# Linformer attention with a max-out FFN on one core: batch 0's k product in one column tile, its prelude reordered, and four output copies moved from ScalarE to VectorE

## The chip, the cores and the metric

The kernel runs on one core of one Trainium2 chip. The metric is the time of one execution in device microseconds. Each run also comes with its span and its mean granted TensorE clock (1.0 is full speed).

"Half clock" below means a stretch in which TensorE's clock is granted at 0.50. In the runs' clock column one such stretch of 3.4 us in 404 us shows as about 0.996. I call a run with a clock under 0.9975 a run with a dip. The clock column has a blind spot: it reads 1.00 until the first recorded change of the clock, so an array that warms up late doesn't count as a dip.

## The reference, cut to what matters

```python
# q, k, v: (8 batches, 8 heads, 1024, 64) fp32; E, F: (64, 1024)
k_proj = np.einsum('ks,bhsd->bhkd', E, k)             # 1024 keys -> 64
v_proj = np.einsum('ks,bhsd->bhkd', F, v)
scores = scale * np.matmul(q, k_proj.transpose(0, 1, 3, 2))
attn = softmax(scores)                                # over the 64
x = np.matmul(attn, v_proj) -> (8192 tokens, 512)
h = np.maximum(np.maximum(x @ w1, x @ w2), x @ w3)    # 512 -> 768
out = h @ w_out                                       # 768 -> 512, fp32
```

The matmuls run in bf16. The three "up" products and the "down" product of the FFN are most of the work: 1152 and 378 matmuls of 512 columns.

## The kernel before

Each batch of 1024 tokens is worked in two chunks of 512. While TensorE multiplies the FFN of one batch, the attention of the next is slipped in between. Batch 0 has nothing to hide behind, so its attention is a prelude: it runs while the first weights are still arriving. The prelude works two "duos" of four heads each for q and k, and four pairs of heads for the values. `idle(n)` issues n fill matmuls whose results nobody reads; they keep the array active. `at(us)` only tells the program's own model of time, which places instructions; it makes no wait on the chip.

```python
    def proj(b, kv, t, heads, width):                 # two 64-column tiles of the array
        for si in range(SI):                          # SI = 8
            for hh in range(2):
                nc.tensor.matmul(
                    out=t[hh * HALF:(hh + 1) * HALF, 0:width],
                    lhsT=efT[:, si, (kv - 1) * KP:kv * KP],
                    rhs=qkv[b][kv][:, heads[hh], si, :],
                    start=(si == 0), stop=(si == SI - 1),
                )
        ...
    def idle(n):
        t, ns = bank()
        for _ in range(n):
            nc.tensor.matmul(out=t, lhsT=warm[:, 0:P], rhs=warm, start=True, stop=True)
        free[ns[0]] = pe(n * MM)
    ...
    def k_duo(u):
        t, ns = bank()
        proj(0, 1, t, (slice(4 * u, 4 * u + 2), slice(4 * u + 2, 4 * u + 4)), 2 * D)
        kp0[u] = att.tile([P, 2 * D], BF16, name="kp0")
        copy("v", kp0[u], t[:, 0:2 * D], ns, 0.3)

    def kt_duo(u):
        ...
        nc.tensor.transpose(out=t[:, 0:P], in_=kp0[u], identity=ident)
        ...
    # the prelude, from the second k duo on
    k_duo(1)
    idle(2)
    kt_duo(1)
    at(14.1)
    v_pair(0)
    for g in (2, 3):
        exps(0, g, *C0, scores(0, g, *C0))
    x(0)
    at(15.5)
    v_pair(1)
    z(2)        # sums, then ln and exp on ScalarE: the softmax's divisor
    z(3)
    x(1)        # values times weights, then the scaling on VectorE: xT
    idle(1)
    at(17.4)
    ...
    # the first FFN chunk: six products w1, ct by ct, with work slipped in
                up_first({
                    (0, 0, 5): [lambda: v_pair(2)],
                    (0, 1, 2): [lambda: x(2)],
                    (0, 1, 5): [lambda: v_pair(3), ld(1)],   # ld(1): load batch 1
                    ...
            # after each chunk: down products; the copy out of PSUM on VectorE or ScalarE
            for tt in range(SPC):
                down(b, ch, tt, "v" if (b, ch) == (0, 0) else "s")
                behind(ch, NJT + tt)
```

The softmax here doesn't subtract the row's maximum and nothing guards it: scores larger than these inputs give would overflow.

## Time and profile before

| | before |
|---|---|
| time of the three timed runs | 405.33, 405.44, 405.68 us |
| time, span, clock of the execution that was traced | 406.75 us, 405.0 us, 0.996 |
| TensorE busy | 392.0 us, 97% |
| first up matmul | 18.97 us |
| half clock | 19.2 to 22.6 us |
| batch 1's first up products wait for their input | 0.67 us at 78.07 us |

The page's summary of the kernel before: span, busy time by engine, then the granted clock in tenths and the busy share of the DMA engines in 40 slices of 10.1 us.

```profile
span 405.0 us, 5872 instructions
PE 392.0 (97%) x2331; PEld 178.8 (44%) x2374; DVE 200.1 (49%) x309; ACT 191.1 (47%) x278; POOL 31.7 (8%) x44
PEclk9989999999999999999999999999999999999999
DMA  9999999948927994991898119950510202020202
```

TensorE is the limit of the whole. In the first eight slices, though, the DMA engines are over 90% busy as well. The 8 in the clock row is most of the half clock.

The timeline of TensorE around the first weights, in the kernel before (start in us, length in us, engine, line, operation, and in brackets how long the engine sat idle before it and what ended that):

```profile
17.42 0.39 PE L380 MATMUL banks<-warm 128*128 128x512 bf16 x1
18.97 2.54 PE L496 MATMUL banks<-xT,w_sb 128*128 128x512 bf16 x6 [1.16 <-DMA w_sb<-in_moe_w_dram]
21.30 1.06 PE L425 MATMUL banks<-v_t,efT 128*128 128x128 bf16 x8
```

L380 is a fill, L496 the up product, L425 a value pair. Six up matmuls take 2.54 us here.

The windows view of the kernel before, by microsecond (columns: length, busy time and count of PE, PEld, DVE, ACT, POOL, then the granted clock, the DMA share and GB/s):

```profile
18.00:19.00 1.00, 0.03 (x1) 0.03 (x2) 0.30 (x1) 0.97 (x2) 0.00 (x0) 1.00 1.23 202
19.00:20.00 1.00, 1.00 (x3) 0.36 (x4) 0.00 (x0) 0.64 (x2) 0.79 (x1) 0.61 1.24 207
20.00:21.00 1.00, 1.00 (x4) 0.42 (x3) 0.00 (x0) 0.00 (x0) 0.63 (x2) 0.50 1.18 209
21.00:22.00 1.00, 1.00 (x9) 0.72 (x8) 0.00 (x0) 0.00 (x0) 0.35 (x2) 0.50 1.16 206
22.00:23.00 1.00, 0.78 (x6) 0.44 (x4) 0.29 (x1) 0.00 (x0) 0.91 (x2) 0.69 1.17 212
```

The timeline of the end of batch 0, kernel before, ScalarE first and then TensorE. L99 is the copy of an output tile, L233 and L239 are the ln and exp of batch 1's divisor.

```profile
71.67 0.59 ACT L99 COPY o_sb<-banks 128x512 f32<-128x512 f32 x1
74.18 0.57 ACT L99 COPY o_sb<-banks 128x512 f32<-128x512 f32 x1
74.64 1.03 ACT L233 ACTIVATE zl<-banks 128x1024 f32<-128x1024 f32 x1
75.70 1.06 ACT L239 ACTIVATE zi<-zl 128x1024 f32<-128x1024 f32 x1
75.30 2.11 PE L496 MATMUL banks<-xT,w_sb 128*128 128x512 bf16 x9
78.07 1.24 PE L496 MATMUL banks<-xT,w_sb 128*128 128x512 bf16 x4 [0.67 <-DVE xT L250]
```

The copies lie in ScalarE's way to the last exp; the scaling on VectorE (L250) follows that exp, and TensorE waits for it.

### The profile page before, as it was taken

How to read it: one execution, taken by the hardware profiler on the slowest of the kernel's cores; microseconds unless marked ns; L12 is line 12 of the kernel's file. 1: busy time of each engine (PE TensorE's matmuls, PEld its weight loads, DVE VectorE, ACT ScalarE, POOL GpSimd, SP SyncE). 2: the span in 40 equal slices, each digit the busy share in tenths (PEclk: the TensorE clock that was granted, in tenths of full speed). 3: DMA queues.
4: the chain of work that ended last, by engine and by line, in shares of the span. 5: the costliest groups of instructions: out<-in, count | busy, mean ns of one | idle time of the engine just before them, and what ended most of it. 6: DMA issues, size and time to landing. Idle time of an engine off the chain costs nothing.

```text
span 405.0 us, 5872 instructions
## 1 busy us (share of the span) xinstructions
PE 392.0 (97%) x2331; PEld 178.8 (44%) x2374; DVE 200.1 (49%) x309; ACT 191.1 (47%) x278; POOL 31.7 (8%) x44
## 2 busy tenths in 40 slices
PE   7899999999999999999999999999999999999996
PEld 3444444344444535444544445444544444444443
DVE  2337764462655527537353655625464363525251
ACT  2611538724763366555544555437535556432322
POOL 7340010002000100200200002000000000000000
PEclk9989999999999999999999999999999999999999
DMA  9999999948927994991898119950510202020202
GB/s 151 206 206 207 229 198 184 232 106 124 256 36 209 177 238 106 141 247 29 211 188 178 49 29 238 205 154 2 139 71 1 104 2 104 2 104 0 105 0 104
DMA packets 62667, 53.33 MB, mean 132 GB/s; under 512 B 30128, under 2 KB 58288, under 8 KB 62640
## 3 DMA queue, kind: packets, MB, share of 16 engines
q0 software_dynamic: 28512, 28.31, 43.8%
q1 hardware_dynamic: 33984, 24.51, 19.5%
q8 instruction: 18, 0.29, 0.3%
q10 hardware_dynamic: 144, 0.13, 0.1%
q14 instruction: 9, 0.07, 0.1%
HBM read 57.15 MB, written 16.78 MB: 183 GB/s over the span
## 4 chain that ended last, share of the span: by engine, by line
PE 89%; DMA 4%; ACT 2%; issue 2%; POOL 1%; DVE 1%; ACTq 0%; DVEq 0%; POOLq 0%
PE banks L496 61%; PE banks L593 19%; PE banks L220 4%; PE banks L284 3%; DMA w_sb<-in_moe_w_dram 3%; PE banks L200 2%; DVE xT L250 1%; ACT zl L233 1%; ACT zi L239 1%; DMA out_dram<-o_sb 0%; POOL k_t L147 0%; ACT pT L211 0%; PE banks L425 0%; POOL q_t L152 0%; POOL v_t L147 0%
## 5 line engine op out<-in xcount | busy, mean ns | idle before, releaser
L496 PE MATMUL banks<-xT,w_sb 128*128 128x512 bf16 x1120 | 256.1, 380 | 4.3 <-DMA w_sb<-in_moe_w_dram 1.2
L496 PEld LDWEIGHTS <-w_sb 128*128 128x128 bf16 x1152 | 109.9, 98 | 139.2 <-issue 12.3
L558 DVE TENSOR_TENSOR m<-banks,h1s 128x512 f32<-128x512 f32 x90 | 62.1, 689 | 85.1 <-ACT h1s L554 52.7
L554 ACT COPY h1s<-banks 128x512 f32<-128x512 f32 x90 | 52.5, 583 | 89.8 <-PE banks L496 87.7
L593 PE MATMUL banks<-wout_sb,hT 128*128 128x512 bf16 x369 | 84.6, 379 | 1.0 <-issue 0.6
L250 DVE TENSOR_TENSOR xT<-banks,zi 128x1024 bf16<-128x1024 f32 (+1 forms) x36 | 39.8, 1106 | 76.1 <-ACT zi L239 54.6
L506 DVE TENSOR_TENSOR hT<-banks,m 128x512 bf16<-128x512 f32 x90 | 62.3, 692 | 10.7 <-PE banks L496 1.2
L99 ACT COPY o_sb<-banks 128x512 f32<-128x512 f32 (+1 forms) x60 | 34.8, 581 | 52.4 <-PE banks L593 52.4
L593 PEld LDWEIGHTS <-hT 128*128 128x128 bf16 x378 | 36.0, 98 | 45.3 <-issue 2.9
L233 ACT ACTIVATE zl<-banks 128x1024 f32<-128x1024 f32 (+1 forms) x36 | 33.5, 931 | 30.6 <-PE banks L220 29.7
L211 ACT ACTIVATE pT<-banks 128x1024 bf16<-128x1024 f32 (+1 forms) x36 | 33.2, 931 | 14.3 <-PE banks L200 14.3
L239 ACT ACTIVATE zi<-zl 128x1024 f32<-128x1024 f32 (+1 forms) x36 | 34.6, 962 | 1.1
L189 POOL DMA_DIRECT2D q_t<-in_q_dram x7 | 6.2, 880 | 204.3 <-DMA qT<-q_p 142.0
L284 PEld LDWEIGHTS <-efT 128*64 128x64 bf16 x256 | 12.8, 110 | 4.5 <-issue 4.0
L220 PE MATMUL banks<-pT,ones 64*64 64x512 bf16 (+1 forms) x144 | 13.9, 376 | 0.7 <-DVE xT L250 0.3
L200 PE MATMUL banks<-qT,kpT 64*64 64x512 bf16 (+1 forms) x144 | 13.3, 358 | 0.4 <-DVE m L558 0.3
L220 PE MATMUL banks<-pT,vp 64*64 64x512 bf16 (+1 forms) x144 | 13.3, 356 | 0.1
L99 DVE CAST vp<-banks 64x256 bf16<-64x256 f32 (+1 forms) x18 | 7.1, 396 | 9.0 <-PE banks L425 5.2
L220 PEld LDWEIGHTS <-ones 64*64 64x64 bf16 x144 | 4.4, 103 | 14.6 <-issue 14.2
L99 DVE COPY q_p<-q_t 128x1024 bf16<-128x1024 bf16 x28 | 10.0, 420 | 0.0
L380 PE MATMUL banks<-warm 128*128 128x512 bf16 x22 | 8.2, 499 | 1.5 <-DVE warm L170 1.2
L284 PE MATMUL banks<-k_t,efT 128*64 128x256 bf16 (+1 forms) x144 | 8.7, 263 | 0.7 <-DMA k_t<-in_k_dram 0.7
(46 smaller groups left out, 94.6 us busy)
## 6 DMA issues: line engine op xcount, KB each, us to landing
out_dram<-o_sb SPq DMA_DIRECT2D x30, 512.0 KB, 3.0
q_t<-in_q_dram POOLq DMA_DIRECT2D x7, 1024.0 KB, 9.6
k_t<-in_k_dram POOLq DMA_DIRECT2D x7, 1024.0 KB, 13.9
v_t<-in_v_dram POOLq DMA_DIRECT2D x7, 1024.0 KB, 19.8
w_sb<-in_moe_w_dram POOLq DMA_DIRECT2D x5, 384.0 KB, 12.4
k_t<-in_k_dram POOLq DMA_DIRECT2D x2, 512.0 KB, 8.7
v_t<-in_v_dram POOLq DMA_DIRECT2D x4, 256.0 KB, 12.0
wout_sb<-in_moe_w_out_dram POOLq DMA_DIRECT2D x1, 768.0 KB, 15.7
```

What stands on the lines that cost most here:

```text
L99: done = {"v": nc.vector.tensor_copy, "s": nc.scalar.copy, "g": nc.gpsimd.tensor_copy}[eng](out=o, in_=i)
L211: nc.scalar.activation(out=pTs[b, g, lo], in_=t, func=AF.Exp, scale=scale)
L220: nc.tensor.matmul(out=t[hp * HALF:(hp + 1) * HALF, c, 0:nsi * HALF], lhsT=w(rows, hp), rhs=p[rows, hp, :], start=True, stop=True,)
L233: nc.scalar.activation(out=zl, in_=t, func=AF.Ln)
L239: nc.scalar.activation(out=zi, in_=zl, func=AF.Exp, scale=-1.0)
L250: nc.vector.tensor_tensor(out=xTs[b][:, g, lo:lo + nsi, :].rearrange("a (c s) p -> a c (s p)", c=2), in0=t, in1=zi, op=ALU.mult,)
L284: nc.tensor.matmul(out=t[hh * HALF:(hh + 1) * HALF, 0:width], lhsT=efT[:, si, (kv - 1) * KP:kv * KP], rhs=qkv[b][kv][:, heads[hh], si, :], ...
L496: nc.tensor.matmul(out=h, lhsT=w_sb[i][:, ct, jt * P:(jt + 1) * P], rhs=xTs[b][:, ct, ch * SPC:(ch + 1) * SPC, :], start=(ct == first), st ...
L506: nc.vector.tensor_tensor(out=o, in0=h, in1=other, op=ALU.max)
L554: nc.scalar.copy(out=h1s, in_=h[0][0])
L558: nc.vector.tensor_tensor(out=m12, in0=h[1][0], in1=h1s, op=ALU.max)
L593: nc.tensor.matmul(out=o_ps, lhsT=hTs[b, ch][:, jt, tt * P:(tt + 1) * P], rhs=wout_sb[:, jt, :], start=(jt == 0), stop=(jt == NJT - 1),)
```

## The change

The intent: the k product of batch 0 issues half the matmuls, value pair 0 covers the wait between the k product and its transpose, fewer fills are needed, and ScalarE is relieved of four output copies at the end of batch 0.

```diff
     def k_duo(u):
         t, ns = bank()
-        proj(0, 1, t, (slice(4 * u, 4 * u + 2), slice(4 * u + 2, 4 * u + 4)), 2 * D)
-        kp0[u] = att.tile([P, 2 * D], BF16, name="kp0")
-        copy("v", kp0[u], t[:, 0:2 * D], ns, 0.3)
+        for si in range(SI):
+            nc.tensor.matmul(
+                out=t[0:KP, 0:4 * D], lhsT=efT[:, si, 0:KP],
+                rhs=k_t[:, 4 * u:4 * u + 4, si, :],
+                start=(si == 0), stop=(si == SI - 1),
+            )
+        pe(0.9)
+        kp0[u] = att.tile([KP, 4 * D], BF16, name="kp0")
+        copy("v", kp0[u], t[0:KP, 0:4 * D], ns, 0.45)
     def kt_duo(u):
...
-        nc.tensor.transpose(out=t[:, 0:P], in_=kp0[u], identity=ident)
+        for gg in range(2):
+            nc.tensor.transpose(
+                out=t[:, gg * KP:(gg + 1) * KP],
+                in_=kp0[u][:, gg * P:(gg + 1) * P], identity=ident[0:KP, 0:KP],
+            )
...
-    idle(11)
+    idle(10)
...
-    idle(5)
+    idle(4)
...
     k_duo(1)
-    idle(2)
+    idle(1)
+    at(14.8)
+    v_pair(0)
     kt_duo(1)
-    at(14.1)
-    v_pair(0)
+    x(0)
     for g in (2, 3):
         exps(0, g, *C0, scores(0, g, *C0))
-    x(0)
-    at(15.5)
+    at(16.1)
     v_pair(1)
+    idle(1)
+    x(1)
     z(2)
     z(3)
-    x(1)
-    idle(1)
-    at(17.4)
+    at(18.2)
...
-                down(b, ch, tt, "v" if (b, ch) == (0, 0) else "s")
+                down(b, ch, tt, "v" if b == 0 else "s")
```

## The prediction

> **What bounds it.** The page gives TensorE 97% of a 405.0 us span, and its granted clock is full (the windows view: 1.00 over 79 to 400 us, TensorE busy 318.0 of 321 us). The change removes no work there, so only the first 80 us can give anything. Three losses there:
>
> 1. Waiting for weights. The timeline has the last fill matmul end at 17.81 us; the first up matmul starts at 18.97 us, after 1.16 us of waiting for the DMA of the first half of w1. The chain of waits gets there through that DMA, not the k products.
> 2. A half clock. The windows view grants 0.61, 0.50, 0.50, 0.69 in the four microseconds from 19 to 23 us: half speed from about 19.22 to 22.62 us, 3.40 us long. The Trainium skill, "TensorE: Matmul & The Clock Gate", section "Part 1: The HAM clock gate", has an activity window of 3413 ns and a halved clock after an idle one; the trace agrees on length and factor. So the window 15.81 to 19.22 us was too idle. Cost: 1.7 us.
> 3. The end of batch 0. At 78.07 us TensorE has waited 0.67 us for xT of batch 1 (VectorE), itself behind a full ScalarE: from 70 to 77 us ScalarE carries four output copies (0.57 us each) between exp and ln.
>
> **What the change does.**
> - k product: twice 16 matmuls of 128 columns in two column tiles (0.64 us a set) become twice 8 of 256 in one tile. From the value products (8 of 128 columns, 0.61 us) I estimate 1.05 us a set. The copy grows from 0.29 to about 0.41 us, the transpose becomes two. Each k chain is some 0.5 us longer.
> - Value pair 0 covers the wait for the second copy; fewer fills. TensorE should finish the prelude near 18.4 us instead of 17.8, still before the weights at 18.95. Loss 1 becomes a wait of 0.4 to 0.6 us, and the up matmuls start when they did.
> - Window 15.81 to 19.22 gets more array time: I count columns streamed for 39% of it before and about 50% after; an earlier window with 48% (8.98 to 12.40) kept the full clock. So probably (0.6) the half clock vanishes. Then up to 1.7 us is gained, less about 0.3 because value pair 2 and the next weights land only just in time: about 1.4 us.
> - Output copies: ScalarE reaches the last ln and exp about 0.5 us earlier; VectorE takes four copies of about 0.68 us in its gaps. xT is ready near 77.5 instead of 78.0: the 0.67 us wait falls to about 0.15. Gain 0.5 us.
>
> **Sum.** With the full clock 405.4 - 1.4 - 0.5 = 403.5 us; without it 404.9. Prediction 403.8 us, range 402.9 to 405.4. Faster by over 2%: 0.01; within 2%: 0.98; slower: 0.01.
>
> **Right or wrong in the profile.** First up matmul at 18.9 to 19.0 us; k product sets near 1.05 us; granted clock 1.00 from 19 to 23 us; the wait for batch 1's xT (near 76 us) under 0.3 us; the same durations from 80 us on.
>
> **What would make it wrong.** The half clock stays (then about 404.9), or moves earlier, since two fills less leave the window 5.6 to 9.0 us emptier (then the prelude is late and the time over 405.5). The k chain passes 18.95 us. The last xT waits behind an output copy on VectorE. Weights or batch 1's values land too late for the gained time.

## More of the kernel before

All runs come from six sittings, five of them on chips whose number is on record (14, 15, 9, 12 and 3). The kernel before was run again in each, and only run times of one sitting are compared; traces are read across sittings.

## The result, and the profile after

The kernel after ran four times: 405.02, 405.19, 405.51 and 406.20 us, median 405.35 us. The kernel before beside it has a median of 405.56 us over four (405.33 to 405.76). The ratio is 0.9998, with a 95% interval of 0.9981 to 1.0016: the same time.

The forecast was 1.6 us less; 0.2 us less was measured. Yet the trace after looks like the forecast come true. The page's summary of the kernel after:

```profile
span 403.2 us, 5841 instructions
PEclk9999999999999999999999999999999999999999
DMA  9999999959907994991799029950510202020202
```

The span fell from 405.0 to 403.2 us and the half clock is gone. The timeline of TensorE around the first weights, kernel after (L506 is now the up product, L435 the value pair):

```profile
18.06 0.39 PE L220 MATMUL banks<-pT,ones 64*64 64x256 bf16 x8
19.54 1.47 PE L506 MATMUL banks<-xT,w_sb 128*128 128x512 bf16 x6 [1.08 <-DMA w_sb<-in_moe_w_dram]
20.84 0.61 PE L435 MATMUL banks<-v_t,efT 128*128 128x128 bf16 x8
```

The up products start 0.57 us later than in the trace before, still waiting for the weights, and six of them take 1.47 us instead of 2.54. The windows view of the kernel after has the clock at 1.00 there:

```profile
19.00:20.00 1.00, 0.47 (x3) 0.23 (x4) 0.05 (x1) 0.94 (x3) 0.22 (x1) 1.00 1.25 209
20.00:21.00 1.00, 1.00 (x8) 0.53 (x7) 0.00 (x0) 0.96 (x2) 1.00 (x2) 1.00 1.17 206
```

The end of batch 0, kernel after: VectorE, then TensorE.

```profile
74.28 0.68 DVE L99 COPY o_sb<-banks 128x512 f32<-128x512 f32 x1
75.28 1.23 DVE L250 TENSOR_TENSOR xT<-banks,zi 128x1024 bf16<-128x1024 f32 x1 [0.32 <-ACT zi L239]
76.42 0.68 DVE L99 COPY o_sb<-banks 128x512 f32<-128x512 f32 x1
74.29 2.10 PE L506 MATMUL banks<-xT,w_sb 128*128 128x512 bf16 x9
76.56 2.75 PE L506 MATMUL banks<-xT,w_sb 128*128 128x512 bf16 x11 [0.17 <-DVE xT L250]
```

The wait for batch 1's xT fell from 0.67 to 0.17 us, and no output copy delays the scaling. So between these two traces 1.8 us were gained, by the mechanisms forecast (though not in the sizes: by the second reading below, 0.97 us before batch 1's value product, where 1.4 was forecast, and 0.8 us after it, where 0.5 was). Between the timed runs 0.2 us were gained. The two can only agree if the traced execution before was not one like its timed runs. The runs' own figures say so: the traced one took 406.75 us with a clock of 0.996, the timed ones 405.33 to 405.68 us. (The clocks of these three timed runs are not on record; later sittings record them.)

A second reading of all traces helps with what follows. From the value product of batch 1 (near 56 us) to its first up product 18.3 us pass in every trace quoted here. From there to the end 329.7 us pass with batch 0's copies on ScalarE and 328.9 us with them on VectorE (329.2 in one of these, h1). So a trace's span is: the start of that value product, plus 18.3 us, plus one of the two numbers. Before: 56.98 + 18.3 + 329.7 = 405.0. After: 56.01 + 18.3 + 328.9 = 403.2.

### The profile page after: what moved, and what is told of

Its sections match the earlier page's. It is cut to its first block, busy times and chain, and to the rows that moved or that the text cites. A ratio compares the mean times of both kernels' runs of the same rounds, so it can differ in the third digit from the quotient of the medians.

```text
span 403.2 us, 5841 instructions
## 1 busy us (share of the span) xinstructions
PE 389.6 (97%) x2314; PEld 178.0 (44%) x2357; DVE 203.1 (50%) x313; ACT 189.4 (47%) x274; POOL 31.6 (8%) x44
## 4 chain that ended last, share of the span: by engine, by line
PE 82%; DMA 11%; ACT 2%; POOL 1%; DVE 1%; issue 1%; DVEq 0%; ACTq 0%; POOLq 0%
PE banks L506 56%; PE banks L603 18%; DMA v_t<-in_v_dram 7%; PE banks L220 4%; DMA w_sb<-in_moe_w_dram 3%; PE banks L284 3%; PE banks L200 2%; DVE xT L250 1%; ACT zi L239 1%; ACT zl L233 1%; DMA out_dram<-o_sb 0%; POOL k_t L147 0%; POOL q_t L152 0%; POOL v_t L147 0%; PE banks L435 0%
## 5 line engine op out<-in xcount | busy, mean ns | idle before, releaser
L506 PE MATMUL banks<-xT,w_sb 128*128 128x512 bf16 x1119 | 254.9, 379 | 3.7 <-DMA w_sb<-in_moe_w_dram 1.1
L506 PEld LDWEIGHTS <-w_sb 128*128 128x128 bf16 x1152 | 109.4, 98 | 138.1 <-issue 10.7
L99 ACT COPY o_sb<-banks 128x512 f32<-128x512 f32 (+1 forms) x56 | 32.6, 581 | 52.2 <-PE banks L603 52.1
L284 PEld LDWEIGHTS <-efT 128*64 128x64 bf16 x224 | 11.6, 110 | 3.3 <-issue 2.7
L99 ACT CAST vp<-banks 64x256 bf16<-64x256 f32 x14 | 5.1, 365 | 8.8 <-PE banks L284 8.6
L380 PE MATMUL banks<-warm 128*128 128x512 bf16 x19 | 7.0, 498 | 1.2 <-DVE warm L170 1.2
## 6 DMA issues: line engine op xcount, KB each, us to landing
v_t<-in_v_dram POOLq DMA_DIRECT2D x7, 1024.0 KB, 18.8
```

The costliest lines, as they stand in the source:

```text
L99: done = {"v": nc.vector.tensor_copy, "s": nc.scalar.copy, "g": nc.gpsimd.tensor_copy}[eng](out=o, in_=i)
L284: nc.tensor.matmul(out=t[hh * HALF:(hh + 1) * HALF, 0:width], lhsT=efT[:, si, (kv - 1) * KP:kv * KP], rhs=qkv[b][kv][:, heads[hh], si, :], ...
L506: nc.tensor.matmul(out=h, lhsT=w_sb[i][:, ct, jt * P:(jt + 1) * P], rhs=xTs[b][:, ct, ch * SPC:(ch + 1) * SPC, :], start=(ct == first), st ...
```

## The experiments

Two theories stand against each other.

- **The base was wrong.** The half clock happened in the execution that was traced but in few of the timed ones, before and after alike. There was little to remove. What is left is the copies' gain and whatever the new prelude costs.
- **The gain was given back.** The half clock was typical before, the change removes it, and the new prelude loses about as much elsewhere, for example by later weights.

All medians and ratios are in one table; the text after it goes run by run. No ratio is beyond 2%; the differences below are finer than that. "Dips" counts runs with a clock under 0.9975. The median of the kernel before in the same sitting stands in the third column.

| run | median us | before us (chip) | ratio [95%] | dips |
|---|---|---|---|---|
| b1_before_again | 405.39 | 405.37 (14) | 0.9992 [0.9975, 1.0008] | 1 of 6 |
| a1_after_again | 405.38 | 405.37 (14) | 0.9989 [0.9972, 1.0006] | 3 of 6 |
| o1_copies_only | 404.80 | 405.37 (14) | 0.9981 [0.9965, 0.9996] | 1 of 6 |
| k1_prelude_only | 405.77 | 405.37 (14) | 1.0005 [0.9989, 1.0021] | 0 of 6 |
| q1_quads_only | 405.98 | 405.21 (15) | 1.0004 [0.9986, 1.0023] | see text |
| r1_order_only | 405.62 | 405.21 (15) | 0.9999 [0.9981, 1.0017] | 0 of 6 |
| f1_copies_and_fills | 404.75 | 405.21 (15) | 0.9979 [0.9960, 0.9998] | 0 of 6 |
| g1_value2_later | 405.09 | 405.21 (15) | 0.9985 [0.9969, 1.0002] | 0 of 6 |
| h1_after_ln_first | 405.84 | 405.38 (9) | 1.0008 [0.9994, 1.0023] | 0 of 6 |
| d1_thin_fills | 404.60 | 405.38 (9) | 0.9985 [0.9968, 1.0002] | 3 of 6 |
| q2_quads_only | 405.55 | 405.38 (9) | 1.0004 [0.9986, 1.0022] | 0 of 6 |
| f2_copies_and_fills | 404.74 | 405.38 (9) | 0.9980 [0.9963, 0.9996] | 0 of 6 |
| p1_after_small_fills | 404.27 | 405.58 (12) | 0.9976 [0.9960, 0.9992] | 1 of 6 |
| p2_after_all_small | 404.90 | 405.58 (12) | 0.9984 [0.9972, 0.9996] | 0 of 5 |
| s2_copies_all_small | 404.54 | 405.58 (12) | 0.9977 [0.9964, 0.9990] | 0 of 5 |
| s3_copies_early_small | 404.69 | 405.58 (12) | 0.9978 [0.9966, 0.9990] | 1 of 5 |
| a2_after_third | 405.24 | 405.98 (3) | 0.9979 [0.9966, 0.9993] | 0 of 5 |
| p3_after_small_fills | 405.49 | 405.98 (3) | 0.9986 [0.9974, 0.9999] | 0 of 5 |

### b1_before_again: the kernel before, unchanged

No edit.

> The kernel before, unedited, run as if it were a new one. Theory A (chance): the half clock near 19 to 23 us falls in some executions of either kernel and misses others, because the window's phase moves against the program; the traced execution of before (406.75 us, mean clock 0.996) was such a one and its timed runs (405.33 to 405.76 us) were not. Then a clock below 1.0 goes with a time near 406.5 us and appears in a minority of these runs, the rest read clock 1.0 and about 405.4 us. Theory B (my prediction): before always has the half clock; then every run of it reads a clock near 0.996 at about 405.4 us.

It is the same program, and its ratio reads 0.9992: differences of 0.1% (0.4 us) are at the edge of what a sitting resolves. Its trace had the full clock and a span of 403.4 us, 1.6 us less than the traced execution that the prediction was built on. In the five sittings the kernel before had a dip in 5 of 53 runs, and b1 in 1 of 6. So the half clock costs the median of the kernel before nothing; at about one run in ten and 1.3 us a dip (406.75 less 405.44) it costs the mean about 0.12 us, by estimate from these numbers. The five dips themselves agree: they took 0.2 to 1.9 us, on average 1.3 us, more than the median of the runs without a dip in their sittings.

### a1_after_again: the kernel after, unchanged

No edit.

> The kernel after, unedited. Theory A: the same minority of runs with clock near 0.996, 1.0 to 1.5 us longer; the other runs 0.3 to 0.5 us shorter than runs of before at clock 1.0, which is the wait for batch 1's xT alone: ratio 0.9988 to 0.9995. Theory B: all runs at clock 1.0 and at least 1.4 us (0.35%) faster than before. Theory C (the prelude costs something): runs at full clock equal to before although the wait for xT is gone, ratio 1.000.

Three of six runs had a dip: 405.51, 405.61 and 405.96 us, against 404.67, 405.00 and 405.25 us without: 0.7 us more on average, and half of the runs where theory A had said a minority and 1.0 to 1.5 us. The traced execution had one too, but at another place. The windows view of this run:

```profile
9.00:10.00 1.00, 1.00 (x7) 0.40 (x4) 0.89 (x2) 0.57 (x1) 0.00 (x0) 0.58 1.38 197
10.00:11.00 1.00, 1.00 (x4) 0.28 (x3) 0.00 (x0) 0.00 (x0) 0.16 (x1) 0.50 1.33 200
11.00:12.00 1.00, 1.00 (x7) 0.82 (x6) 0.00 (x0) 0.00 (x0) 0.41 (x1) 0.50 1.27 207
12.00:13.00 1.00, 1.00 (x5) 0.26 (x3) 0.36 (x1) 0.00 (x0) 0.54 (x1) 0.71 1.27 210
```

Half clock from about 9.2 to 12.6 us: the k product of this execution takes 1.92 us in place of 1.03. The change does not remove the half clock. Over all its runs the kernel after had one in 4 of 15 (1 of 4, 3 of 6, 0 of 5), no rarer than before. This is the first theory's case: there was hardly a half clock in the base to remove, and no sign that the change makes it rarer. Under the second theory most runs of the kernel before would have shown a clock near 0.996.

### o1_copies_only: the copies alone

```diff
-                down(b, ch, tt, "v" if (b, ch) == (0, 0) else "s")
+                down(b, ch, tt, "v" if b == 0 else "s")
```

> Before, with only the output copies of batch 0's second chunk on VectorE. Theory A and C: wait of TensorE for xT before the last slice of batch 1's first matmuls 0.1 to 0.2 us instead of 0.67; time 0.4 to 0.5 us less, ratio 0.9988 to 0.9990; the half clock as often as in before. Theory B: the half clock stays in every run.

404.80 us, ratio 0.9981, an interval that leaves 1 out. From batch 1's first up product to the end 329.70 us (before), 329.68 (b1), 329.63 (k1), 329.68 (r1) and 329.68 (q2) pass with the copies on ScalarE; 328.94 (o1), 328.94 (f1), 328.91 (after), 328.98 (a1), 328.90 (g1) and 328.96 (a2) with them on VectorE. That is 0.74 us, the same each time. The wait for xT accounts for 0.50 of it (0.67 to 0.17 us).

The other 0.24 us lie 230 us later. The chain of waits in b1 has a gap there:

```profile
306.90 1.52 PE banks L496 x7
308.43 0.38 issue
308.80 0.70 DVE hT L506
```

VectorE begins a max 0.38 us after its inputs are ready, for no wait that the profile shows, and a down product waits for it. In o1 the same max follows at once, and its 24 down matmuls take 5.34 us where b1's take 5.58. The timelines of TensorE in b1 and then in o1:

```profile
308.25 5.58 PE L593 MATMUL banks<-wout_sb,hT 128*128 128x512 bf16 x24
307.88 5.34 PE L593 MATMUL banks<-wout_sb,hT 128*128 128x512 bf16 x24
```

It is so in each of the traces compared: k1 and r1 have the gap (5.58 and 5.60 us), f1, d1, after and a1 do not (5.34 us). A hint at the cause: a transfer of 8 KB on an instruction queue (q14, probably that of VectorE, since more instructions on VectorE bring its transfers forward) starts at 309.5 to 310.3 us in the three with copies on ScalarE, right after the gap, and at 305.6 to 307.1 us in the five with copies on VectorE. Four more instructions on VectorE (313 in place of 309) shift where such a transfer falls. This is argued from eight traces, not tested.

### k1_prelude_only: all of the change but the copies

```diff
-                down(b, ch, tt, "v" if b == 0 else "s")     # the kernel after
+                down(b, ch, tt, "v" if (b, ch) == (0, 0) else "s")
```

> After, with the output copies of batch 0's second chunk back on ScalarE, so only the prelude is changed. Theory A: ratio 1.000 within 0.0005. Theory B: 1.4 us faster, 0.9965. Theory C: 0.3 to 0.5 us slower, 1.0008 to 1.0012, with the first up matmul or the weights' landing later than in before.

405.77 us, ratio 1.0005, against 0.9992 for the unchanged program on the same chip. The prelude gains nothing and probably loses a few tenths. Its trace shows one way of losing them. The timeline of TensorE and of ScalarE in k1:

```profile
18.50 0.39 PE L220 MATMUL banks<-pT,ones 64*64 64x256 bf16 x8
18.82 1.74 PE L506 MATMUL banks<-xT,w_sb 128*128 128x512 bf16 x6
20.82 0.61 PE L435 MATMUL banks<-v_t,efT 128*128 128x128 bf16 x8 [0.26 <-ACT zl L233]
20.17 0.60 ACT L233 ACTIVATE zl<-banks 128x512 f32<-128x512 f32 x1
```

The same place in o1, which has the old prelude:

```profile
17.42 0.39 PE L380 MATMUL banks<-warm 128*128 128x512 bf16 x1
18.77 1.47 PE L496 MATMUL banks<-xT,w_sb 128*128 128x512 bf16 x6 [0.95 <-DMA w_sb<-in_moe_w_dram]
20.07 0.61 PE L425 MATMUL banks<-v_t,efT 128*128 128x128 bf16 x8
18.41 0.60 ACT L233 ACTIVATE zl<-banks 128x512 f32<-128x512 f32 x1
```

In k1 the weights were there when the prelude ended; it wins no time by it. Its prelude ends 1.1 us later, so the last ln of pairs 2 and 3 ends at 20.77 us instead of 19.01 and still holds its bank of PSUM (the buffer that matmuls write to) when value pair 2 wants one. The first six up matmuls take 1.74 us instead of 1.47, value pair 2 waits 0.26 us, and the stretch from the first up product to the second q transposes takes 14.50 us instead of 13.80. This costs 0.7 us where the weights come early (k1, a2) and nothing where they come late (after, 13.80 us from a start at 19.54); early and late here mean before and after the end of the prelude. Either way the later of the two, weights or prelude, sets the pace: the loss of the new prelude was hidden in the trace after behind weights that happened to come late. That the bank is the reason is read from the waits; g1 and h1, below, tried to remove this wait and gained nothing that can be told apart from noise.

Not all of the 1.1 us is the new order, though. The fills and the first k product, in k1 and then in o1:

```profile
8.51 1.89 PE L380 MATMUL banks<-warm 128*128 128x512 bf16 x4
10.33 1.17 PE L409 MATMUL banks<-k_t,efT 128*64 128x256 bf16 x8
```

```profile
9.74 0.64 PE L284 MATMUL banks<-k_t,efT 128*64 128x128 bf16 x16 [0.51 <-DMA k_t<-in_k_dram]
```

In k1 four fills take 1.89 us, because the array is cold until 10.6 us (fills step at 0.427 us instead of 0.216; in o1 it is cold until 7.2 us), and the k product begins 0.59 us later than in o1. The clock column shows 0.999 for this run. Of the 19 traces with a clock record only k1 and p2 (10.1 us) warm up this late, and both have the new prelude; the count of dips misses them. So the prediction's risk that fewer fills leave the early window emptier is larger than the dips alone say, though two traces give no rate.

### q1_quads_only and q2_quads_only: the k product by quads (four heads in one column tile), the old order

```diff
     def k_duo(u):
         t, ns = bank()
-        proj(0, 1, t, (slice(4 * u, 4 * u + 2), slice(4 * u + 2, 4 * u + 4)), 2 * D)
+        for si in range(SI):
+            nc.tensor.matmul(out=t[0:KP, 0:4 * D], lhsT=efT[:, si, 0:KP], ...)
...                                   # and the two transposes; all else as before
```

> Before with only the k product by quads (one column tile, two transposes per copy); order, fills and output copies as before. Theory C1 (the longer k chain delays exp and ln on ScalarE and so the prelude, which then ends after the weights have landed): each k set 1.05 us instead of 0.64, its copy 0.42 instead of 0.29, first ln of pairs 2 and 3 about 0.8 us later than in the traces of before with full clock, and 0.3 to 0.5 us slower, ratio 1.0007 to 1.0012. Rival C2 (the new order and the fewer fills are what costs): ratio 1.000.

> The same kernel as the quads-only run, whose profiled execution ran at the half clock from end to end and can't be read. C1: the sets at 1.05 us, ln of pairs 2 and 3 some 0.8 us later than before, first up matmul to the second q transposes 14.2 to 14.5 us unless the weights come late; median 0.3 to 0.7 us above before, as the other 5 runs (405.98 against 405.21 us) suggest. C2: no difference from before.

The traced execution of q1 was useless for its purpose: it ran at half clock from end to end. The groups view, up matmuls, q1 and then q2 (the same kernel on another chip); columns as on the page: count, busy us, mean ns, idle before.

```profile
span 819.8 us, 5886 instructions
L506 PE MATMUL banks<-xT,w_sb 128*128 128x512 bf16 x1152 | 544.5, 676 | 0.0
```

```profile
L506 PE MATMUL banks<-xT,w_sb 128*128 128x512 bf16 x1152 | 257.9, 379 | 1.0 <-DVE xT L250 0.7 <-DMA w_sb<-in_moe_w_dram 0.2
```

821.54 us, once; its other five runs took 405.37 to 406.12 us (clocks of 0.998 to 1.0), and these make the ratio of 1.0004. The clock column says 1.0 for the 821.54 us run and its page has no clock row, so only the durations give it away. Run again as q2: 405.55 us, 1.0004, no such execution. Quads alone gain nothing. In its trace the k products of 1.03 to 1.06 us (0.64 before) leave no mark in the stretch: up at 18.81 us, second q transposes at 32.62 us.

### r1_order_only: the new order and fills, the old k product

It is k1 with the k product and transpose of the kernel before put back.

> After's order, fills and start times with before's k product (two column tiles) and before's output copies. C1: ratio 1.000 or a little under, the first up matmul waits for the weights' DMA again. C2: 0.3 to 0.5 us slower, ratio 1.0007 to 1.0012, and the first fills or transposes at the slow step more often.

405.62 us, ratio 0.9999. The trace starts the up products at 19.31 us after a wait of 1.03 us for the weights. So neither half of the prelude gains alone, and there is no hidden winner among them.

### f1_copies_and_fills and f2_copies_and_fills: the copies, the old prelude, three more fills

```diff
     x(1)
-    idle(1)
+    idle(4)                          # o1 with the wait for the weights filled
     at(17.4)
```

> Output copies on VectorE, before's prelude, and three more fill matmuls in the wait for the first weights (four instead of one, 0.65 us more work in about 1.0 us of wait). Theory A says that the half clock is a matter of how busy a 3.4 us window is: no run of this kernel then reads a clock of 0.996 for a dip near 19 to 23 us, and the median is the 404.7 us of the full-clock runs with the copies on VectorE, ratio about 0.998. Rival: fills do not change the dip; then one run in five reads 0.996 as in before. If the fills delay the first up matmul, 0.1 to 0.3 us slower than with the copies alone.

> The same kernel as the run with copies on VectorE and three more fills, again, as the best so far: median 404.6 to 404.9 us, ratio 0.998, no run with clock under 0.998.

404.75 us on chip 15 and 404.74 us on chip 9, ratios 0.9979 and 0.9980, no dip in 12 runs. This is the best version that I can vouch for: 0.2% (0.8 us) under the kernel before, twice, with an interval that leaves 1 out each time. The kernel after was not run in these two sittings; against the kernel before it averages 0.9989, so this version is probably ahead of it too, by about 0.1%, and a variant of each kind in one sitting agrees (o1 404.80 us, a1 405.38 us on chip 14). It is hardly better than o1 without the fills (0.9981), as it must be if dips are rare. That no run of 12 had a dip shows little by itself: at the 5 in 53 of the kernel before, 12 runs show none about three times in ten.

### d1_thin_fills: o1 with thin fills in the second half of the prelude

```diff
     k_duo(0)
-    idle(2)
+    idle(2, 64)                      # 64 columns in place of 512; so with all eight fills from here on
```

> Output copies on VectorE and before's prelude, with the seven fill matmuls after the first k product cut from 512 to 64 columns, 1.3 us less streaming. Theory A (a quiet 3.4 us window halves the clock): most runs read a clock of 0.996 or less and the median is 0.5 to 1.5 us above the 404.8 us of the copies alone, and the windows view shows the half clock for 3.4 us. If fills have no part in it, the clock is below 0.997 in at most one run of six and the time is 404.8 us.

(By the edit the thinned fills are eight, about 1.5 us of streaming, and not seven.) Three of six runs had a dip (404.38, 405.16 and 405.98 us), against 0 of 12 for f1 and f2. So the fullness of the fills seems to bear on the half clock, which is the mechanism of the prediction; with six runs, and with the kernel after ranging from 0 of 5 to 3 of 6 unchanged, it is a pointer, and neither proof nor a rate. And the median is 404.60 us, as low as that of f2 beside it. One of its runs with a dip took 404.38 us. Presumably a dip costs little where TensorE would wait for data anyway; no trace of such a run was taken.

### g1_value2_later: the kernel after, value pair 2 placed two up matmuls later

```diff
-                    (0, 0, 5): [lambda: v_pair(2)],
-                    (0, 1, 2): [lambda: x(2)],
+                    (0, 1, 1): [lambda: v_pair(2)],
+                    (0, 1, 4): [lambda: x(2)],
```

> After, with value pair 2 issued two up matmuls later and its use too, so that it does not wait for the bank that ScalarE's last ln of the prelude frees. If that wait (0.26 us in a trace of the changed prelude) is the cost, the wait before value pair 2 is gone and the time is 0.2 to 0.3 us less than after, ratio near 0.998 to 0.9985. If the delay only moves to the next wait for xT, the time stays as after.

405.09 us, 0.9985, not told apart from the kernel after. The wait for ScalarE's ln is gone from its trace, and value pair 3 waits 0.48 us for VectorE instead; the stretch takes 14.23 us. The wait moved.

### h1_after_ln_first: the kernel after, both ln ahead of both exp

```diff
-    z(2)
-    z(3)
+    z_two((2, 3))                    # ln, ln, exp, exp; zl0 in two buffers
```

> After, with the two ln of value pairs 2 and 3 issued before the two exp that follow them on ScalarE, so that the second ln ends about 0.63 us sooner and gives its bank to value pair 2 sooner. Theory C3 (the changed prelude costs because ScalarE's ln, late by 0.8 us, holds the banks of the first up matmuls and of value pair 2): the stretch from the first up matmul to the transposes of q's second half is 13.8 us also in a trace in which the weights do not come late, where it was 14.5; time 0.2 to 0.5 us under after's, near 404.9 us, ratio near 0.998. Rival (the cost lies in the k chain or in late weights): the time stays at 405.3 to 405.4 us.

405.84 us, 1.0008: no help. In its trace the weights came late (up at 19.84 us), so the thing that it should mend was not in the way. It neither confirms nor refutes the ln wait as a cost.

### p1_after_small_fills, p2_after_all_small, s2_copies_all_small, s3_copies_early_small, p3_after_small_fills: the same fills in smaller pieces

The trace has a transfer of 16 KB on the instruction queue, 0.97 us long. It comes at 15.4 to 16.7 us with the old prelude and at 17.3 to 17.8 us with the whole new one (18.8 in a1, which ran at half clock before), just ahead of the first weights. If it delays them, more (and smaller) fill matmuls of the same total length should move it. p1 and p3 are one kernel: the kernel after with its first ten fills in 40 pieces. p2 is the kernel after with all fills in pieces. s2 is o1 with all fills in pieces, s3 is o1 with the first 16 in pieces.

```diff
-    idle(10)
+    idle(10, 128)                    # p1, p3: four matmuls of 128 columns for one of 512
```

> After, with the first ten fill matmuls of 512 columns cut into forty of 128, the same streaming with 60 more instructions. Theory D (the instruction transfer in front of the first weights delays them): the transfer moves from 17.5 to about 15 us, the first up matmul starts at 18.7 to 19.1 us again or as soon as the prelude ends, and the time is 0.3 to 0.5 us under after's, near 404.9 us, ratio near 0.9985. Rival (weights land by chance, or by the order of the work): the first up matmul at 19.3 to 19.8 us, time 405.4 us.

> After, with all fills in pieces of 128 columns (about 110 more instructions before the weights). Theory D: the transfer near 12 to 13 us, the rest as for p1: first up matmul at 18.7 to 19.1 us, near 404.9 us. Rival: as after.

> The copies on VectorE with before's prelude, all fills in pieces of 128 columns: 138 more instructions, so that the second instruction transfer comes near 17 to 18 us. Theory D: the weights land at 19.3 to 19.8 us instead of 18.8, and the time is 0.4 to 0.7 us above the copies alone: 405.2 to 405.5 us. Rival: 18.8 us and 404.8 us.

> The same with only the fills before the k product cut small: 96 more instructions, the first transfer near 12 us, the second near 20 us or later. Control for s2. Theory D: weights at 18.7 to 19.0 us, time 404.6 to 404.9 us. If cutting the fills itself costs, both s2 and s3 are slower.

> After with the first ten fills in pieces of 128 columns, again. If the edit is worth what the first run suggests: 0.4 to 1.0 us under the run of after beside it, instruction transfer near 15.4 us, first up matmul at 18.6 to 19.1 us. If the first run was luck of the chip or of the loads: the same time as after within 0.3 us.

p1 was the fastest of all at 404.27 us, and s2 missed its aim (the transfer came at 11.5 and 21.8 us). It tells something all the same: with no such transfer in between, its up products still waited for the weights until 19.47 us, against 18.77 us in o1. The repeat of p1 as p3 took 405.49 us on chip 3, with a ratio of 0.9986 where p1 had 0.9976. The gain did not repeat. The idea that this transfer is the main cause of later weights is not supported, and what moves the weights' arrival from 18.4 to 19.9 us between executions stays open.

### a2_after_third: the kernel after, once more

No edit.

> After, unedited, beside p1 again on one chip. Median 405.2 to 405.5 us, instruction transfer at 17.3 to 17.8 us (later if the clock or the data are late), first up matmul at 19.3 us or later.

405.24 us, ratio 0.9979, no dip in 5. The kernel after has now read 0.9998, 0.9989 and 0.9979; the mean is 0.9989.

Its trace shows where a faster front is returned. The timelines of a2 and then of the kernel after at batch 1's value product:

```profile
56.06 1.06 PE L284 MATMUL banks<-v_t,efT 128*64 128x256 bf16 x16 [0.58 <-DMA v_t<-in_v_dram]
```

```profile
56.01 1.06 PE L284 MATMUL banks<-v_t,efT 128*64 128x256 bf16 x16
```

a2 reached the second q transposes 0.46 us earlier than the kernel after (32.88 against 33.34 us), and then waited 0.58 us for batch 1's values from memory. Both start this product within 0.05 us of each other. In 9 of the 17 traces without a dip TensorE waits there, 0.19 to 0.58 us; the product starts between 55.03 and 56.55 us in all 17. The half clock of the traced execution before pushed it to 56.98 us. The stretch lost 1.68 us to it (15.48 against 13.80 us), but 56.98 is only 1.3 us after what the same prelude otherwise reaches (55.64 us, the median of its seven traces without a dip). So against the other traces even a half clock that really was there is not worth all of its 1.7 us. How much of it comes back depends on when the values land: in the traced execution before they were there at about 55.0 us (issued at 25.8, landed 29.2 us later), so it could have used all 1.7 us; the other seven traces of this prelude have them at 55.2 to 56.0 us. For the new prelude the median of seven such traces (k1, after, a2, g1, p1, p2, p3) is 56.01 us. That is 0.37 us later. (Some of these traces have other fills, and g1 another place for value pair 2; h1, 56.55 us, is left out. The unedited preludes alone, b1 and o1 against k1, after and a2, differ by 0.3 to 0.7 us.) The values land later too, at a median of 56.0 against 55.6 us, so part of the 0.37 us may be theirs.

## Why the prediction was wrong

**What the reasons add up to.** Copies: 0.74 us gained. Prelude: about 0.37 us lost, by medians of seven traces each. Half clock: no change in how often it comes that the runs could show. The sum is -0.37 us, or 0.9991 of the time before, an estimate worked out from the traces; the three ratios of the kernel after average 0.9989. The unchanged kernel before, run against itself, read 0.9992, so the runs alone would not tell the kernel after from it.

**The step that failed** is the sum: "With the full clock 405.4 - 1.4 - 0.5 = 403.5 us". It takes the cost of the half clock, read from a traced execution of 406.75 us, off a median of 405.44 us, whose runs mostly had no half clock. Taken off its own base it comes to 406.75 - 1.4 - 0.5 = 404.85 us, close to the 405.02 us of the traced execution after. The chance of 0.6 that "the half clock vanishes" was asked of the wrong quantity: what matters is how often it comes before (5 of 53 runs) and after (4 of 15). The figures that show it, 406.75 us and a clock of 0.996, were there beforehand. A second term was mis-sized: the prediction let the new prelude cost nothing where the half clock stays ("without it 404.9"), and the traces put that cost at about 0.37 us. That 404.85 us comes close to 405.02 us is partly luck, since in the trace after late weights hid it.

Point by point:

1. *The half clock: its length and factor, and its cause.* Length and factor are right; that too idle a window causes it fits all traces, and d1 points to it, but it is not proven here. The Trainium skill, "TensorE: Matmul & The Clock Gate", section "Part 1: The HAM clock gate (the "warmup" mystery)", gives a window of 3413 ns, a halved clock and a window that runs free of the kernel's start; the traces show 3.41 us, 0.50, and first warm-ups anywhere from 3.9 us (p1) to 10.6 us (k1) after the start. The free-running window is what I cited and did not draw the conclusion from: with a phase that differs by execution, one trace shows one draw.
2. *"moves earlier, since two fills less leave the window 5.6 to 9.0 us emptier".* Seen in a1 (half clock from 9.2 to 12.6 us), and in another form in k1 and p2, whose arrays stay cold until 10.6 and 10.1 us. It had been named as a risk, and it is one.
3. *"Loss 1 becomes a wait of 0.4 to 0.6 us, and the up matmuls start when they did."* Half right. Starts lie at 18.4 to 19.9 us with the new prelude and at 18.8 to 19.6 us with the old, more widely than the 0.1 us I allowed. The new prelude ends later and, in k1 and a2, where the weights were there first, costs 0.7 us in the stretch after (14.50 against 13.80 us), which I had put at 0.3 us and only under the gained half clock.
4. *The k set at 1.05 us.* Right: 1.03 to 1.06 us at full clock. The Trainium skill, "TensorEngine Tiling (Array Packing)", section "Performance Considerations", recommends column tiling for a stationary side of up to 64 columns, and its section "Theoretical Speedup" gives up to 2x; here giving the tiling up made the same product 1.6 times as long (0.64 to 1.03 us).
5. *The copies, 0.5 us.* Right in the mechanism: 0.67 to 0.17 us of wait. It was undersized in the sum, since a further 0.24 us came from a gap on VectorE at 308 us that the prediction did not look for.
6. *"Weights or batch 1's values land too late for the gained time."* It happened: 0.58 us of waiting in a2, in 9 of 17 traces in all. The front of this kernel is limited twice by arriving data, at 19 and at 56 us.

**What stays open.** Executions without a dip still differ by 1 to 2 us (the kernel before took 404.84 to 406.73 us on chip 15), and the traces put most of that before 56 us, in when weights and values arrive. What moves those arrivals was not found; the test with instruction transfers did not settle it. The time of the first warm-up does not order them: batch 1's value product starts at 55.85 us in k1 (warm at 10.6 us) and at 56.06 us in a2 (warm at 4.1 us). Whether the new prelude's 0.37 us is real in every execution is open too: it rests on medians of seven single traces, and k1 against b1 (1.0005 against 0.9992) overlaps.

## What to carry to other kernels

Before taking a loss off a measured time, check that the traced execution is one of those that made the time: compare its own time and clock with the timed runs. A loss whose presence depends on the phase of a free-running window is to be weighed by how often it comes, before as well as after. And look for the next arrival of data behind the stretch that is to get shorter, for it may take the gain back: here the front waited for weights at 19 us and again for values at 56 us, and only the copies, which lie behind both, kept their gain.

## What the Trainium skill lacked or had wrong

- "TensorE: Matmul & The Clock Gate" tells what an idle window does and that the window runs free, but not how often a prelude with gaps of about 1 us throttles. These runs: 5 of 53 for the kernel before, 4 of 15 for the kernel after, 3 of 6 with thin fills, 0 of 12 with three more fills; and two traces of 19 with a first warm-up after 10 us.
- The same page says that activity releases the throttle; its "HAM trace caveats" have a clock stuck for 50 us and more and records that can't be relied on, but no case that lasts a whole execution. One execution of a kernel with TensorE 99% busy ran at half clock from end to end: 821.54 us, up matmuls of 676 ns on average in place of 379. Its clock read 1.0, with no clock row in its profile, which agrees with that caveat.
- No page says that the profile's clock reads 1.00 until its first recorded change, although the array is still cold: before that the fills of 512 columns step at 0.427 us, the figure the Clock Gate page gives for a cold array.
- "Runtime: NRT & Kernel Launch", section "Instruction fetch mechanics", has the refill of instructions in blocks of 16 KiB and calls the cost of a boundary mostly hidden. It has no duration (16 KB in 0.97 us near 16 us here) and does not say whether a refill holds other transfers up; on q14 the transfers here are of 8 KB. The gap of 0.38 us on VectorE at 308 us lies next to one in three traces; no run here shows that it causes it.
